# Two pairs' input loads moved behind a weight piece, and matmul units re-cut, in a linear-attention and MLP kernel

## The chip, the cores and the metric

The kernel runs on one core of a Trainium2 chip. A core has a matrix engine (TensorE, PE in the profile; its weight loads are listed as PEld), VectorE (DVE), ScalarE (ACT), GpSimd (POOL) and SyncE (SP, which only issues DMAs and waits). They run side by side, each through its own instructions in order, and wait for each other by semaphores. Sixteen DMA engines move data between DRAM and the on-chip memory. The metric is the device time of one execution in microseconds (us); less is better.

## The reference

The inputs are q, k, v of shape (4, 8, 768, 64) in float32, a decay `lam` per head, a gain `g_ln` and two weight matrices, W1 (512 x 2048) and W2 (2048 x 512). First comes attention with decay, in blocks of 64 positions with a running state, then a layer norm and a two-layer MLP with a residual:

```python
for b in range(nb):                      # blocks of 64 positions
    intra = einsum('bhic,bhjc->bhij', qb, kb) * Dmask      # Dmask: lam ** (i - j), lower triangle
    intra = einsum('bhij,bhjd->bhid', intra, vb)
    inter = einsum('bhid,bhde->bhie', qb * lam_pow, kv_state)
    out[:, :, sl] = intra + inter
    kv_state = lam_block * kv_state + einsum('bhsd,bhse->bhde', kb * rev_pow, vb)
x = out as (4, 768, 512)
xn = (x - mean) / sqrt(var + 1e-6) * g_ln
result = x + relu(xn @ w_ch1) @ w_ch2
```

## The kernel before

The 4 x 768 positions are cut into twelve windows of 256, numbered 0 to 11; a window is a pair of 128-row tiles, so "the fourth pair" is window 3 and "the fifth" window 4. A window goes through these stages:

- loads of k, q, v (512 KB each) into buffers `kin`, `qin`, `vin`, of which there are three per name; SP issues them (L76, later L80). `open_in` names the buffers; with its second argument true, POOL first writes one element of the k buffer (L91), so that the loads, which write the same buffer, wait for POOL to get that far;
- casts and scalings to bf16 (`in_k`, `in_q`, `in_v`; L218 to L245) on ACT, DVE or POOL;
- transposes of k and q to `kqT`, on PE for windows 0 to 2 (L253), by DMA from SP for the later ones (L260);
- scores (L282), masking, state products (L316), new states (`new_state`; POOL's decay is L322), attention output (L428, L441) and the norm;
- the transpose of the normed rows to `xT`, on PE (L502) or by DMA, and then the MLP of this window, called a group.

The MLP is cut into units. The first product x W1 makes 16 hidden blocks of 128 for the group's two tiles. A whole unit, `m1(n)`, takes two hidden blocks for both tiles: eight matmuls of 256 columns (L539). A split unit, `m1.tile(c, i)`, takes four hidden blocks for tile i alone: sixteen matmuls of 128 columns (L650). Both do the same arithmetic, fill one bank of the accumulation memory and are drained by one ACT instruction (L542, L653). Eight units of either kind make a group. The second product is `m2(i, part)` for groups 0 to 3 (four matmuls of 512 columns, L676), where part 0 to 3 reads piece 0 to 3 of W2; the later groups use a product scheme with fewer multiplications (L574).

W1 and W2 come in four pieces each, cast on the way by DMAs that POOL issues (`load_w1`, L117; `load_w2`, L120). `behind(tile)` is a copy of one column by POOL (L737), so that whatever follows on POOL's queue stands behind the landing of that tile.

The order is written out by hand. Each engine runs its instructions in the order of the program text. `plan` is a list of the units from group 1's second half on, and `units(n)` issues the next n of them between the attention steps. The order around the change, before it: POOL issues the last two pieces of W2, writes the gate element for window 3, scales v of window 2 and decays two states; SP issues k, q, v of window 3 and k, q of window 4; then PE goes through window 2's transposes, the first units of the plan and window 2's scores.

At the start of the program PE does 36 small matmuls into a tile `unread` (L180), whose values nothing reads, in a loop of 18 with two each.

Of the kernel before, what the change touches and what calls it, by code (L numbers as in the profile page):

```python
# [17 lines left out]
def kernel(  # L18
# [11 lines left out]
    nc = tc.nc  # L30
# [41 lines left out]
    def fill(got, name, u, hs, eng=None):  # L72
        eng = eng or nc.sync
        src = dict(k=k, q=q, v=v)[name]
        if u < LB:
            eng.dma_start(got[:, hs], source(src, u, hs))  # L76
            return
        cc, b = divmod(u, B)
        for j in range(2):
            eng.dma_start(got[:, hs, j * D:(j + 1) * D],  # L80
                          src[b, hs, cc * W + j * C:cc * W + (j + 1) * C, :].rearrange("h p d -> p h d"))
# [6 lines left out]
    def open_in(u, gate):  # L88
        qkv_in[u] = {name: inp.tile([128, H, 2 * D], F32, tag=name + "in", name=name + "in") for name in "kqv"}
        if gate:  # L90
            nc.gpsimd.memset(qkv_in[u]["k"][:, 0, 0:1], 0.0)  # L91

    def load_in(u, name, eng):
        got = qkv_in[u][name]
        fill(got, name, u, slice(0, H), eng)
        qkv_in[u][name] = got.rearrange("p h (j d) -> p h j d", j=2)
# [14 lines left out]
    w2 = [const.tile([128, KB // NWC, DM], F16, name=f"w2_{c}") for c in range(NWC)]  # L111
# [7 lines left out]
    def load_w2(c):  # L119
        nc.gpsimd.dma_start(w2[c], moe_w_ch2[c * W2K * 128:(c + 1) * W2K * 128, :].rearrange("(k p) d -> p k d", p=128))  # L120
# [54 lines left out]
    nc.vector.memset(ones, 1.0)  # L175
    nc.vector.tensor_copy(keep64[half[1]], keep64_b[half[1]])
    unread = ps.tile([128, 32], F32, tag="po0", name="unread")
    for _ in range(18):
        for b in range(2):
            nc.tensor.matmul(unread[half[b]], lhsT=ident[half[0], half[b]], rhs=ident[half[0], 0:32],  # L180
                             start=True, stop=True, skip_group_check=True)
# [60 lines left out]
    def in_v(u, eng, hs=ALL):  # L242
        n = hs.stop - hs.start
        lv = lam_v[:, hs, :, None] if u < LB else lam_p[:, 1, hs, None, None]
        eng.tensor_tensor(st[u]["vb"][:, hs], qkv_in[u]["v"][:, hs], lv.to_broadcast([128, n, 2, D]), op=ALU.mult)  # L245
# [75 lines left out]
    def decay(eng, dst, src):  # L321
        eng.tensor_tensor(dst, src, lam_s[:, :, None].to_broadcast([128, NP, D]), op=ALU.mult)  # L322

    def state_sum(u, ab):
        tmp = wk.tile([128, NP, D], F32, tag="Stmp", name="Stmp")
        nc.vector.tensor_tensor(tmp, st[u]["pk"][ab], state[u % B], op=ALU.add)
        return tmp

    def new_state(u, ab, eng):

        s = st[u]
        b = u % B
        if ab == 1 and len(s["pk"]) == 1:
            return
        old = state.get(b)
        if ab == 0:
            s["S"] = [(old, old)]
        Sn = wk.tile([128, NP, D], BF16, tag="S", bufs=12, name="Sn")
        if old is None and eng is nc.scalar:
            for p in range(NP):  # L340
                nc.scalar.activation(Sn[:, p], s["pk"][ab][:, p], ACT.Identity, scale=lam_s[:, p:p + 1])
        elif old is None:
            decay(nc.vector, Sn, s["pk"][ab])
        else:
            tmp = s.pop("tmp", None) or state_sum(u, ab)
            decay(eng, Sn, tmp)
        state[b] = Sn
        if ab == 0:
            s["S"].append((Sn, Sn))
# [384 lines left out]
    def behind(tile_ap):  # L734

        seen_p = wk.tile([128, 1], F32, tag="seen_p", name="seen_p")
        nc.gpsimd.tensor_copy(seen_p, tile_ap)  # L737
# [47 lines left out]
    m1b, m2b = mlp(1)  # L785
# [41 lines left out]
    def s1b(u):  # L827
        scores(u, 0)
        mask(u, 0)
# [194 lines left out]
    keep_x(1, nc.scalar.copy)  # L1024
    load_w2(2)
    load_w2(3)
    open_in(3, True)
    in_v(2, nc.gpsimd)
    load_in(3, "k", nc.sync)
    load_in(3, "q", nc.sync)  # L1030
    load_in(3, "v", nc.sync)
    open_in(4, False)
    load_in(4, "k", nc.sync)
    load_in(4, "q", nc.sync)
    plan = [(m1b.tile, c, i) for c in (2, 3) for i in range(2)]
    plan += [(m2, i, part) for part in range(KB // 4) for m2, i in ((m2a, 0), (m2a, 1), (m2b, 0))]
    plan += [(m2b, 1, part) for part in range(KB // 4)]
    for g in range(2, len(groups)):
        m1, m2 = mlp(g)
        plan += [(m1.tile, 0, 0), (m1.tile, 0, 1)] if g == 2 else [(m1, 0), (m1, 1)]  # L1040
        plan += [(m1, n) for n in range(2, m1.count)]
        if g >= WG:
            plan += [(m2.w, n) for n in range(8)]
        else:
            plan += [(m2, i, part) for i in range(len(groups[g])) for part in range(KB // 4)]
# [3 lines left out]
    def units(n):  # L1049
        for _ in range(n):  # L1050
            f, *a = next(steps)
            f(*a)
# [4 lines left out]
    transpose_pe(2, 1, (0, 1, 2, 3))  # L1057
    new_state(0, 1, nc.gpsimd)
    new_state(1, 1, nc.gpsimd)
    units(2)  # L1060
    s1b(2)
    units(2)
# [310 lines left out]
```

## Time and profile before

| | |
|---|---|
| median of 5 runs | 209.07 us (208.81 to 209.25) |
| the profiled execution | 209.25 us; its span from the first to the last instruction 207.5 us |
| PE | 198.5 us busy (96%), 3199 matmuls |
| PEld | 159.9 us (77%) |
| DVE, ACT, POOL | 133.8 us (65%), 120.7 us (58%), 84.5 us (41%) |
| HBM read and written | 27.27 MB and 6.29 MB, 162 GB/s over the span |
| granted PE clock | 0.997 |

Busy time is the time in which an engine had at least one instruction running. PE's matmuls are pipelined and the profile models their ends, so the time that one matmul takes in a stream is read from start to start and not from its listed length. Times in a timeline row are the start and the length, counted from the first instruction; brackets give the idle time before the row and who ended it. DMA share is the mean busy share of the 16 DMA engines; in a short stretch it can exceed 1, since a packet's whole time is counted where it starts.

### The profile page before, as it was taken

What the parts mean: (1) busy time and instruction counts of PE and PEld (TensorE: products, weight loads), DVE (VectorE), ACT (ScalarE), POOL (GpSimd) and SP (SyncE); (2) the same over time, 40 slices, a digit from 0 to 9 for tenths busy, and PEclk for the clock granted to TensorE, in tenths of its full rate; (3) what the DMA queues carried; (4) which work ended last, traced back from release to release, by engine and by line L of the source; (5) the groups of instructions that cost most, each with busy time, mean ns of one, the idle gap of its engine ahead of it and who ended that gap; (6) DMA issues with size and microseconds to landing.
All of it is one profiled execution on the core that took longest, in us unless ns stands there. A gap on an engine that the chain in (4) does not pass through costs nothing.

```text
span 207.5 us, 7435 instructions
## 1 busy us (share of the span) xinstructions
PE 198.5 (96%) x3199; PEld 159.9 (77%) x3199; DVE 133.8 (65%) x277; ACT 120.7 (58%) x278; POOL 84.5 (41%) x117
## 2 busy tenths in 40 slices
PE   4988999999999999999999999999999999999991
PEld 2477889655785586588888888888888888988881
DVE  2586481525964459867888774766876947865252
ACT  3775578726258358257565775585596565652620
POOL 5658049016946342365264441782282202001020
PEclk9999999999999999999999999999999999999998
DMA  4999999999998999999999999797968020158403
GB/s 106 303 255 212 171 287 174 206 267 274 160 264 216 255 186 180 189 243 197 212 207 121 192 208 160 202 202 153 196 124 176 3 51 0 29 122 269 144 16 90
DMA packets 91011, 36.41 MB, mean 175 GB/s; under 512 B 65121, under 2 KB 88161, under 8 KB 90978
## 3 DMA queue, kind: packets, MB, share of 16 engines
q1 hardware_dynamic: 86368, 31.53, 74.6%
q0 software_dynamic: 4224, 4.19, 12.7%
q8 instruction: 25, 0.41, 0.9%
q10 hardware_dynamic: 386, 0.20, 0.4%
q14 instruction: 8, 0.07, 0.1%
HBM read 27.27 MB, written 6.29 MB: 162 GB/s over the span
## 4 chain that ended last, share of the span: by engine, by line
PE 88%; ACT 3%; DMA 3%; DVE 2%; SPq 1%; issue 1%; POOLq 0%; POOL 0%; DVEq 0%
PE pm L539 36%; PE pm L676 14%; PE pm1t L650 6%; PE pwd L574 6%; PE pwa L574 6%; PE pwc L574 6%; PE pwb L574 3%; DMA qin<-in_q_dram 3%; PE po L441 2%; PE tp L253 2%; PE po L428 2%; PE xt L502 1%; DVE x L587 1%; PE po L415 1%; PE sc L362 1%; PE sc L282 1%
## 5 line engine op out<-in xcount | busy, mean ns | idle before, releaser
L539 PE MATMUL pm<-xT,w 128*128 128x256 bf16 x672 | 76.9, 273 | 0.0
L539 PEld LDWEIGHTS <-w 128*128 128x128 bf16 x672 | 64.6, 98 | 8.3 <-DVE Smid L397 0.3
L542 ACT ACTIVATE hT<-pm 128x512 f16<-128x512 f32 x84 | 49.2, 596 | 24.8 <-PE pm L539 24.7
L676 PE MATMUL pm<-w,hT 128*128 128x512 f16 x128 | 29.8, 380 | 0.0
L574 PEld LDWEIGHTS <-hs 128*128 128x128 f16 x256 | 24.9, 98 | 2.9
L599 POOL TENSOR_TENSOR x<-ev_u,x 128x256 f32<-128x256 f32 x8 | 5.8, 724 | 51.4 <-ACT ev_u L598 40.0
L557 DVE TENSOR_TENSOR hs<-hT 128x1024 f16<-128x1024 f16 x16 | 14.0, 873 | 16.1 <-ACT hT L542 16.0
L322 POOL TENSOR_TENSOR Sn<-Stmp,lam_s 128x256 bf16<-128x256 f32 x16 | 9.8, 616 | 33.3 <-DVE Stmp L400 15.5
L676 PEld LDWEIGHTS <-hT 128*128 128x128 f16 x128 | 11.7, 98 | 12.5
L574 PEld LDWEIGHTS <-hT 128*128 128x128 f16 x192 | 18.8, 98 | 2.2
L469 DVE SCALAR_TENSOR_TENSOR xc<-po,nmean,g_row 128x512 bf16<-128x512 f32 x18 | 13.0, 746 | 4.9 <-ACT nmean L468 4.8
L467 ACT ACTIVATE x<-po 128x512 f32<-128x512 f32 x18 | 10.6, 590 | 7.9 <-PE po L441 4.5
L650 PE MATMUL pm1t<-xT,w 128*128 128x128 bf16 x192 | 13.6, 234 | 0.7 <-ACT kqT L254 0.6
L650 PEld LDWEIGHTS <-w 128*128 128x128 bf16 x192 | 12.5, 106 | 1.7 <-DMA w<-in_moe_w_ch_dram 0.9
L245 POOL TENSOR_TENSOR vb<-vin,lam_v 128x1024 bf16<-128x1024 f32 (+1 forms) x7 | 11.6, 1660 | 5.2 <-DMA vin<-in_v_dram 5.2
L512 ACT ACTIVATE sq<-x,nmean 128x512 bf16<-128x512 f32 x18 | 12.9, 719 | 0.3
L653 ACT ACTIVATE hT<-pm1t 128x512 f16<-128x512 f32 x12 | 7.3, 605 | 9.9 <-PE pm1t L650 9.8
L292 DVE TENSOR_TENSOR mA<-sc,keep 128x512 bf16<-128x512 f32 x14 | 9.0, 684 | 5.1 <-PE sc L282 5.1
L245 POOL TENSOR_TENSOR vb<-vin,lam_p 128x1024 bf16<-128x1024 f32 x6 | 11.4, 1896 | 2.0 <-ACT hT L542 1.9
L587 DVE SCALAR_TENSOR_TENSOR x<-pwd,rstd,x 128x256 f32<-128x256 f32 x16 | 7.7, 482 | 3.6 <-POOL x L607 3.6
L239 POOL TENSOR_TENSOR kq<-qin,lam_p 128x512 bf16<-128x512 f32 x9 | 9.3, 1042 | 1.7 <-DMA qin<-in_q_dram 1.7
L587 DVE SCALAR_TENSOR_TENSOR x<-pwa,rstd,x 128x512 f32<-128x512 f32 (+1 forms) x16 | 9.1, 612 | 0.8
(134 smaller groups left out, 317.2 us busy)
## 6 DMA issues: line engine op xcount, KB each, us to landing
out_dram<-x SPq DMA_DIRECT2D x22, 256.0 KB, 3.9
w<-in_moe_w_ch_dram POOLq DMA_DIRECT2D x8, 512.0 KB, 8.3
kin<-in_k_dram SPq DMA_DIRECT2D x14, 256.0 KB, 5.6
qin<-in_q_dram SPq DMA_DIRECT2D x14, 256.0 KB, 4.9
vin<-in_v_dram SPq DMA_DIRECT2D x14, 256.0 KB, 4.8
kin<-in_k_dram SPq DMA_DIRECT2D x5, 512.0 KB, 7.9
qin<-in_q_dram SPq DMA_DIRECT2D x5, 512.0 KB, 6.6
vin<-in_v_dram SPq DMA_DIRECT2D x5, 512.0 KB
```

The costliest lines, as they stand in the source:

```text
L245: eng.tensor_tensor(st[u]["vb"][:, hs], qkv_in[u]["v"][:, hs], lv.to_broadcast([128, n, 2, D]), op=ALU.mult)
L322: eng.tensor_tensor(dst, src, lam_s[:, :, None].to_broadcast([128, NP, D]), op=ALU.mult)
L467: nc.scalar.activation(x, po, ACT.Copy, accum_out=sm)
L469: nc.vector.scalar_tensor_tensor(xc, in0=po, scalar=nm, in1=g_row, op0=ALU.add, op1=ALU.mult)
L512: nc.scalar.activation(sq, s["x"][:, ab], ACT.Square, bias=s["nmean"][:, ab:ab + 1], accum_out=ss[:, ab:ab + 1])
L539: nc.tensor.matmul(pm[:, b, :], lhsT=w1[n // W2K][:, kk, (n % W2K) * 128:(n % W2K + 1) * 128], rhs=xT_of[g][:, kk, 0:N], start=(b == 0 and ...
L542: nc.scalar.activation(hT[:, u * NB:(u + 1) * NB, 0:N], pm, ACT.Relu)
L557: nc.vector.tensor_tensor(s13, b[:, :, 1:2, :].to_broadcast([128, n, 2, 128]), b[:, :, 0:4:3, :], op=ALU.subtract)
L574: nc.tensor.matmul(pr[bank], lhsT=lhs(r), rhs=rhs, start=(first and r == 0), stop=(r == KB // 2 - 1), skip_group_check=True)
L587: nc.vector.scalar_tensor_tensor(out, in0=in0, scalar=r[ab], in1=in1, op0=ALU.mult, op1=ALU.add)
L650: nc.tensor.matmul(pm[:, b, :], lhsT=w1[c][:, kk, b * 128:(b + 1) * 128], rhs=xT_of[g][:, kk, i * 128:(i + 1) * 128], start=(b == 0 and kk ...
L676: nc.tensor.matmul(acc[i], lhsT=hT[:, kk, i * 128:(i + 1) * 128], rhs=w2[kk // W2K][:, kk % W2K, :], start=(kk == 0), stop=(kk == KB - 1))
```

## The change

It has three parts.

- The loop of `unread` runs 16 times instead of 18: 32 matmuls instead of 36.
- The plan's units are cut otherwise. Group 1's second half was four split units and becomes four whole ones. Group 2's first two units were split and become whole. Group 3's last four units were whole and become split. The number of units stays the same.
- The gate and the loads of window 3 and of k and q of window 4 move down in the text, behind window 2's transposes, the first unit and POOL's two state decays, and a `behind` is put before them, so that on POOL's queue the gate stands behind the landing of W2's second piece. `in_v(2)` stays ahead of it. The definition of the plan moves up, which has no effect of its own.

```diff
-    for _ in range(18):
+    for _ in range(16):
         for b in range(2):
             nc.tensor.matmul(unread[half[b]], ...
...
     load_w2(2)
     load_w2(3)
+    in_v(2, nc.gpsimd)
+    plan = [(m1b, n) for n in range(m1b.count // 2, m1b.count)]
+    plan += [(m2, i, part) for part in range(KB // 4) for m2, i in ((m2a, 0), (m2a, 1), (m2b, 0))]
+    plan += [(m2b, 1, part) for part in range(KB // 4)]
+    for g in range(2, len(groups)):
+        m1, m2 = mlp(g)
+        if g == 3:
+            plan += [(m1, n) for n in range(4)] + [(m1.tile, c, i) for c in (2, 3) for i in range(2)]
+        else:
+            plan += [(m1, n) for n in range(m1.count)]
...
+    transpose_pe(2, 0, (0, 1, 2, 3), nc.vector)
+    units(1)
+    transpose_pe(2, 1, (0, 1, 2, 3))
+    new_state(0, 1, nc.gpsimd)
+    new_state(1, 1, nc.gpsimd)
+    behind(w2[1][:, 0, 0:1])
     open_in(3, True)
-    in_v(2, nc.gpsimd)
     load_in(3, "k", nc.sync)
     load_in(3, "q", nc.sync)
     load_in(3, "v", nc.sync)
     open_in(4, False)
     load_in(4, "k", nc.sync)
     load_in(4, "q", nc.sync)
-    plan = [(m1b.tile, c, i) for c in (2, 3) for i in range(2)]
...
-        plan += [(m1.tile, 0, 0), (m1.tile, 0, 1)] if g == 2 else [(m1, 0), (m1, 1)]
-        plan += [(m1, n) for n in range(2, m1.count)]
...
-    transpose_pe(2, 0, (0, 1, 2, 3), nc.vector)
-    units(1)
-    transpose_pe(2, 1, (0, 1, 2, 3))
-    new_state(0, 1, nc.gpsimd)
-    new_state(1, 1, nc.gpsimd)
     units(2)
     s1b(2)
```

More of the change, by code (lines that the diff above doesn't have):

```diff
@@ L1026 @@
     load_w2(3)
-    open_in(3, True)
     in_v(2, nc.gpsimd)
[L1029 to L1034, printed above, removed]
-    plan = [(m1b.tile, c, i) for c in (2, 3) for i in range(2)]
+    plan = [(m1b, n) for n in range(m1b.count // 2, m1b.count)]
     plan += [(m2, i, part) for part in range(KB // 4) for m2, i in ((m2a, 0), (m2a, 1), (m2b, 0))]
@@ L1059 @@
     new_state(1, 1, nc.gpsimd)
+    behind(w2[1][:, 0, 0:1])
+    open_in(3, True)
+    load_in(3, "k", nc.sync)
+    load_in(3, "q", nc.sync)
+    load_in(3, "v", nc.sync)
+    open_in(4, False)
+    load_in(4, "k", nc.sync)
+    load_in(4, "q", nc.sync)
     units(2)
```

## The prediction

> **What bounds the kernel now.** I read the page first, then the list of what TensorE (PE) waited for, then the timelines of PE, GpSimd (POOL) and SyncE (SP) around the edit, then the DMA share in stretches of 2 us.
>
> From the page: the span, and the shares of the chain that ended last.
>
> ```profile
> span 207.5 us, 7435 instructions
> PE 88%; ACT 3%; DMA 3%; DVE 2%; SPq 1%; issue 1%; POOLq 0%; POOL 0%; DVEq 0%
> ```
>
> PE is the chain. Its waits over the whole run (waiter, releaser, us in total, times, longest):
>
> ```profile
> PE g_all L183 <- DMA g_one<-in_moe_g_ln_dram: 1.6, 1, 1.6
> PE unread L180 <- POOL ident L132: 1.4, 1, 1.4
> PE pm1t L650 <- ACT kqT L254: 0.6, 1, 0.6
> ...
> ```
>
> Three more rows of 0.2 each close that list, and all six waits lie before 17 us. From 17 to 197 us PE waits for nothing the list resolves, so this change can help only by removing PE work or by changing what happens in the first 22 us, and can hurt only by making PE wait for something that now comes in time.
>
> PE around the edited units (start, length, line, shape, count):
>
> ```profile
> 35.03 1.95 PE L650 MATMUL pm1t<-xT,w 128*128 128x128 bf16 x32
> 36.91 0.42 PE L282 MATMUL sc<-kqT 64*64 64x128 bf16 x16
> ...
> 54.38 1.95 PE L650 MATMUL pm1t<-xT,w 128*128 128x128 bf16 x32
> 56.17 1.91 PE L539 MATMUL pm<-xT,w 128*128 128x256 bf16 x16
> ...
> ```
>
> The 32 matmuls of two split units (L650) start at 54.38 and hand over at 56.17: 1.79 us, 55.9 ns each, 0.895 us a unit. Further on, 32 matmuls of four whole units (L539) start at 76.65 and hand over at 80.16: 3.51 us, 0.878 a unit. Split and whole units cost PE almost the same.
>
> POOL, on whose queue the new wait goes:
>
> ```profile
> 31.90 1.55 POOL L120 DMA_DIRECT2D w<-in_moe_w_ch_dram  x2
> 33.43 0.12 POOL L91 MEMSET kin<- 128x1 f32 x1
> 33.49 1.92 POOL L245 TENSOR_TENSOR vb<-vin,lam_v 128x1024 bf16<-128x1024 f32 x1
> 35.36 1.18 POOL L322 TENSOR_TENSOR Sn<-Stmp,lam_s 128x256 bf16<-128x256 f32 x2
> 41.84 0.61 POOL L322 TENSOR_TENSOR Sn<-Stmp,lam_s 128x256 bf16<-128x256 f32 x1 [5.30 <-DVE rstd L517]
> ```
>
> SP, which issues the moved loads:
>
> ```profile
> 33.58 0.37 SPq L76 DMA_DIRECT2D kin<-in_k_dram  x1
> ...
> 34.77 7.60 SPq L76 DMA_DIRECT2D vin<-in_v_dram  x1
> 42.46 3.55 SPq L76 DMA_DIRECT2D kin<-in_k_dram  x1
> 46.06 1.55 SPq L76 DMA_DIRECT2D qin<-in_q_dram  x1
> 48.45 5.30 SPq L260 DMA_TRANSPOSE kqT<-kq  x2
> ```
>
> The 7.60 and 3.55 us are issues held back by transfers that do not drain. The stretches (last two columns: DMA share, GB/s) say why:
>
> ```profile
> 34.00:36.00 2.00, 2.00 (x40) 2.00 (x38) 0.58 (x1) 2.00 (x5) 2.00 (x3) 1.00 1.18 177
> 36.00:38.00 2.00, 2.00 (x48) 1.80 (x45) 0.63 (x2) 1.51 (x3) 0.54 (x1) 1.00 1.15 188
> 42.00:44.00 2.00, 2.00 (x79) 1.10 (x77) 0.00 (x0) 0.00 (x0) 0.46 (x1) 1.00 1.19 215
> 46.00:48.00 2.00, 2.00 (x18) 1.02 (x19) 0.78 (x2) 0.89 (x3) 0.62 (x2) 1.00 1.22 306
> ```
>
> The DMA engines are full (share over 1) from 32 to 52 us. The rate shows what runs: about 183 GB/s while W2 moves alone (its rate is counted in its half-width destination), about 306 with the q/k/v loads alone, 215 when mixed.
>
> **The change, part by part.** The sum is made against the profiled execution, 209.25 us (span 207.5 plus 1.75 around it). The median of the five runs is 209.07, so I take 0.18 off.
>
> *Unread matmuls, 36 to 32.* They run 1.43 to 2.57 us, a pair every 0.053 us: 2 pairs, 0.11 us less. PE then sits idle 1.55 us for g_one until 4.12, which hides it: 0. Without that cover it would be a gain of 0.11.
>
> *Split against whole units.* The four units of m1b and the first two of group 2 become whole, the last four of group 3 become split: six fewer, four more, net two. 2 x (0.895 - 0.878) = -0.03 us. ScalarE drains one 128x512 bank per unit either way (605 ns split at L653, 596 whole at L542). A whole unit needs both halves of xT: group 1's transposes ran at 27.3 and 29.5, against a unit at 33.69; group 2's at 47.9 and 49.0, against 54.38. No wait. Splitting group 3's second half leaves its W2 products fed: the first of them needs hidden blocks 0 to 3, from units 0 and 1.
> The Trainium skill, "TensorE: Matmul & The Clock Gate", section "Back-to-back issue gap", gives about 81 ns a matmul for N=128 in a real stream of weight loads and matmuls; an estimate by that page makes a split unit 16 x 81 = 1.30 us and the net saving 0.84 us, the sum 208.2. The row above measures 55.9 ns, and the sum goes by the row.
>
> *POOL's order.* in_v(2) starts 0.06 earlier, the two state decays end at 36.5, then POOL waits for W2's second piece. That piece is issued at 29.94 and, by the view of tile w, lands 7.9 later, at 37.8; nothing ahead of it changes. The copy takes 0.19 (the same copy at L737), the gate memset 0.12: 38.1. Next on POOL's queue is the decay at 41.84, which waits for VectorE anyway. The cover is 3.7 us, so: 0. If W2's piece came later than 41.5, PE's use of that state at 43.84 would be late by the excess less 1.4.
>
> *The loads on SP.* SP reaches them at 38.2 instead of 33.58. Behind them in its queue are only the transposes of the fourth pair at 48.45 (they wait for VectorE's half of k) and what follows. The first k load is issued at 33.58 and, by the view of tile kin, lands 12.6 later, at 46.2. But at 34 to 38 us the rate is that of W2 alone (177, 188): the early issue gets it nothing until about 37. From 38 to 44 the mix of 215 splits as 183f + 306(1-f), f = 0.74: a quarter of the engines' time is the loads', about 80 GB/s. Holding them until their first packets, some 2 us after 38.2, takes 3 us x 0.26 = 0.8 us of engine time from them and gives it to W2, whose last piece then lands 0.8 earlier (33.45 - 0.75 + 13.3 = 46.0 now). The engines never run dry, so the loads get it back: k lands between 46.2 (all given back) and 47.0 (none). I take 46.3, as the full share in all stretches is nearest to the first. The other four loads stand behind it in the same full pipe and shift no more.
> The Trainium skill, "DMA: Bandwidth & Descriptors", section "Queues, rings and completion order", says that each DMA engine takes turns between the queues that have work. By that, an estimate is that the loads had half the engines from 35 us on, and the delay would be some 2 us, which still leaves the sum where it is. The rows of 34 to 38 us do not show such turns.
>
> *What a later k meets.* By the view of tile kqT the transposes land at 55.0 and 55.7 (issued 48.45 and 52.46, landing 6.5 and 3.3 later) and PE's scores of this pair start at 58.28: 2.5 us of slack. For the fifth pair they land at 66.7 and scores start at 70.51: 3.8. So 0 to 0.8 us later costs 0. W2's pieces were not waited for either: the third lands at 42.0 and is first read at about 45, the fourth at 46.0 and is read at 48.11; landing earlier is worth 0.
>
> Sum: 209.25 - 0.03 - 0.18 = 209.04, so **209.0 us**. With the bounds (0.11 at the start, 0.2 either way for run to run, which is half the 0.44 between the fastest and slowest run) the likeliest case covers 208.7 to 209.4.
>
> **The rivals.**
>
> *Late loads (slower).* If issue order did decide and the loads moved by the whole 4.6 us, k lands at 50.8. The first transpose then starts 0.42 (VectorE's copy) later at 51.3 instead of 48.45, 2.8 late; the pair's q is cast on POOL (2.22 us for two), which puts the second transpose up to 4.6 late, landing at 58.5 to 60.3 against 58.28. PE stalls 0.2 to 2.0 us there, and SP's later loads follow. Price: 209.3 to 211.1, middle 210.2. It decides once the transposes slip more than 2.5 us. Against it: the 34-to-38 rows. For it: SP's queue is serial and hardly idle after 48 us.
>
> *The first 22 us (either side).* The first two L650 units take 1.89 and 1.82 us, later ones 0.9: PE runs at half pace until about 22.0. No row shows what ends it. If the four missing matmuls move that point, each us is worth 0.5 us. PE's stretch without a wait starts at 16.7, so at the earliest the gain is 5.3 / 2 = 2.6 us; I price it at one us either way of a likely move of 2: 208.0 or 210.0. PE's 0.64 us idle before 16.73, where the weight loads wait for W1's first piece, is of the same kind, within 0.6. Against it: the removed 0.11 us lies 14 us ahead of that stretch, behind another idle time.
>
> *Split units cost more than their start times show (faster).* Each has 8 extra weight loads of 98 ns. If these were exposed, two units fewer give 2 x 8 x 0.098 = 1.6 us: 207.5. Against it: 55.9 ns from start to start already contains them.
>
> *The change does nothing* is, in time, my forecast.
>
> **How the numbers follow.** A measurement of this kernel can tell about 0.2% (0.4 us) from no change. Forecast 0.50 (same). Late loads 0.17, slower. First 22 us later 0.08, slower; earlier 0.17, faster. Split units 0.08, faster. So faster 0.25, same 0.50, slower 0.25. The range leaves out the 0.08 below and the upper half of the late loads above: 208.0 to 210.2.
>
> **What would show it.** In the new profile: on POOL a copy ending near 38.0 and the memset after it; on SP the first k load at 38.2, landing 8 to 9 us later; W2's last piece landing near 45; the transposes within 1 us of 48.45 and 52.46; PE's wait list still without a row behind 17 us; whole units at 33.7 to 37 of 0.88 us. Wrong would be: a PE wait for kqT, vb or DMA between 57 and 90 us (late loads), or the first full-pace matmul more than 0.4 us away from 22.0.

## The result, and the profile after

The changed kernel takes 209.99 us (median of 39 runs, 208.61 to 212.66) against 208.99 us (median of 65 runs, 207.66 to 210.31) for the one before: ratio 1.0048, 95% interval 1.0035 to 1.0061. It is 1.0 us slower. Here and below, ratios leave out executions in a slower state of the chip; of this kernel's these are the ones of 212.43 and 212.66 us, and without them the slowest took 211.11. The profiled execution took 210.21 us with a span of 208.5.

The page of the changed kernel, span and PE's share:

```profile
span 208.5 us, 7396 instructions
PE 198.0 (95%) x3179; PEld 158.9 (76%) x3179; DVE 132.4 (64%) x277; ACT 120.9 (58%) x278; POOL 84.7 (41%) x118
```

PE works 0.5 us less and the span is 1.0 us longer, so PE stands somewhere. Its list of waits has one new row that matters:

```profile
PE g_all L183 <- DMA g_one<-in_moe_g_ln_dram: 1.7, 1, 1.7
PE unread L180 <- POOL ident L132: 1.4, 1, 1.4
PE pm L539 <- DVE Smid L397: 1.3, 1, 1.3
```

It is the only row behind 17 us, and the timeline puts it at 149 us, 110 us after the edit of the loads. First PE, then its weight loads, around it:

```profile
148.02 1.05 PE L539 MATMUL pm<-xT,w 128*128 128x256 bf16 x8
150.34 6.29 PE L539 MATMUL pm<-xT,w 128*128 128x256 bf16 x56 [1.27 <-DVE Smid L397]
...
150.33 6.01 PEld L539 LDWEIGHTS <-w 128*128 128x128 bf16 x56 [1.54 <-issue]
```

Eight matmuls of a whole unit start at 148.02, 0.109 us apart, so the ninth was due at 148.90. It starts at 150.34: 1.43 us lost, from start to start. The same place in the profile of before has no such hole:

```profile
148.61 2.56 PE L539 MATMUL pm<-xT,w 128*128 128x256 bf16 x22
```

Two things in these rows speak against the named releaser. The weight load reads only W1, which landed 120 us earlier, and it stands too, put down to "issue": no semaphore in the profile explains it. And VectorE's `Smid` (149.34 to 149.76 in its timeline), which could have freed the new unit's bank, ends 0.58 us before PE goes on.

Up to there the changed kernel was ahead. The first L676 unit behind group 3's first product starts at 79.78 (80.16 before): 0.38 ahead. Of that, 0.34 was there at the first full-pace matmul (21.72 against 22.06), which is an accident of the execution (the last section has its range over all profiles), and 0.04 is what the re-cut saves. 1.43 - 0.38 = 1.05 us is the loss in the span.

The rest of the profile answers point by point to what was shown of before. POOL, the new wait and its cover:

```profile
33.42 1.92 POOL L245 TENSOR_TENSOR vb<-vin,lam_v 128x1024 bf16<-128x1024 f32 x1
35.29 1.18 POOL L322 TENSOR_TENSOR Sn<-Stmp,lam_s 128x256 bf16<-128x256 f32 x2
37.59 0.18 POOL L737 CAST seen_p<-w 128x1 f32<-128x1 f16 x1 [1.11 <-DMA w<-in_moe_w_ch_dram]
37.70 0.10 POOL L91 MEMSET kin<- 128x1 f32 x1
41.42 0.61 POOL L322 TENSOR_TENSOR Sn<-Stmp,lam_s 128x256 bf16<-128x256 f32 x1 [3.62 <-DVE rstd L517]
```

SP, the moved loads and the transposes behind them:

```profile
37.83 0.37 SPq L76 DMA_DIRECT2D kin<-in_k_dram  x1
...
48.03 4.75 SPq L260 DMA_TRANSPOSE kqT<-kq  x2
```

k is issued 4.25 us later and lands 8.3 us after that (12.6 before), at 46.1 against 46.2. The transposes start 0.4 earlier than before. W2's last piece lands at 44.4 instead of 46.0. This part cost nothing, as forecast. One step on the way was other than worked out: the first packet of k moves 3.8 us after the issue (37.83 to 41.59), where some 2 us were taken, and in the kernel before it was 3.6 us (33.58 to 37.19). So the empty wait moved along with the loads.

### The profile page after: what moved, and what is told of

Its sections match the earlier page's. It is cut to its first block, busy times and chain, and to the rows that moved or that the text cites. A ratio compares the mean times of both kernels' runs of the same rounds, so it can differ in the third digit from the quotient of the medians.

```text
span 208.5 us, 7396 instructions
## 1 busy us (share of the span) xinstructions
PE 198.0 (95%) x3179; PEld 158.9 (76%) x3179; DVE 132.4 (64%) x277; ACT 120.9 (58%) x278; POOL 84.7 (41%) x118
## 4 chain that ended last, share of the span: by engine, by line
PE 85%; ACT 3%; issue 3%; DMA 3%; DVE 2%; POOL 1%; SPq 1%; POOLq 0%; DVEq 0%; ACTq 0%
PE pm L539 36%; PE pm L676 14%; PE pwc L574 5%; PE pwa L574 5%; PE pm1t L650 5%; PE pwd L574 5%; PE pwb L574 3%; DMA qin<-in_q_dram 3%; PE po L441 2%; PE tp L253 2%; PE po L428 2%; PE xt L502 1%; DVE x L587 1%; PE sc L282 1%; PE po L415 1%
## 5 line engine op out<-in xcount | busy, mean ns | idle before, releaser
L539 PE MATMUL pm<-xT,w 128*128 128x256 bf16 x688 | 79.2, 273 | 1.3 <-DVE Smid L397 1.3
L539 PEld LDWEIGHTS <-w 128*128 128x128 bf16 x688 | 66.0, 98 | 10.2 <-issue 1.5
L542 ACT ACTIVATE hT<-pm 128x512 f16<-128x512 f32 x86 | 50.9, 597 | 31.8 <-PE pm L539 31.7
L676 PE MATMUL pm<-w,hT 128*128 128x512 f16 x128 | 29.8, 380 | 0.0
L557 DVE TENSOR_TENSOR hs<-hT 128x1024 f16<-128x1024 f16 x16 | 12.7, 796 | 19.0 <-ACT hT L542 19.0
L676 PEld LDWEIGHTS <-hT 128*128 128x128 f16 x128 | 11.7, 98 | 12.5
L574 PEld LDWEIGHTS <-hT 128*128 128x128 f16 x192 | 18.8, 98 | 2.2
L650 PE MATMUL pm1t<-xT,w 128*128 128x128 bf16 x160 | 11.0, 234 | 0.7 <-ACT kqT L254 0.6
L650 PEld LDWEIGHTS <-w 128*128 128x128 bf16 x160 | 10.3, 106 | 1.4 <-DMA w<-in_moe_w_ch_dram 0.9
L574 PE MATMUL pwa<-w,hT 128*128 128x256 f16 x64 | 9.6, 273 | 0.0
```

The costliest lines, as they stand in the source:

```text
L539: nc.tensor.matmul(pm[:, b, :], lhsT=w1[n // W2K][:, kk, (n % W2K) * 128:(n % W2K + 1) * 128], rhs=xT_of[g][:, kk, 0:N], start=(b == 0 and ...
L542: nc.scalar.activation(hT[:, u * NB:(u + 1) * NB, 0:N], pm, ACT.Relu)
L557: nc.vector.tensor_tensor(s13, b[:, :, 1:2, :].to_broadcast([128, n, 2, 128]), b[:, :, 0:4:3, :], op=ALU.subtract)
L574: nc.tensor.matmul(pr[bank], lhsT=lhs(r), rhs=rhs, start=(first and r == 0), stop=(r == KB // 2 - 1), skip_group_check=True)
L650: nc.tensor.matmul(pm[:, b, :], lhsT=w1[c][:, kk, b * 128:(b + 1) * 128], rhs=xT_of[g][:, kk, i * 128:(i + 1) * 128], start=(b == 0 and kk ...
L676: nc.tensor.matmul(acc[i], lhsT=hT[:, kk, i * 128:(i + 1) * 128], rhs=w2[kk // W2K][:, kk % W2K, :], start=(kk == 0), stop=(kk == KB - 1))
```

## The cause, as the experiments will show it

PE's instructions come from DRAM in packets of 16 KB on a DMA queue that the page calls "q8 instruction": 25 packets, 0.41 MB, in both kernels. That the queue is PE's is worked out from the count: a matmul is two instructions, the weight load and the multiplication, and 3199 matmuls of the kernel before are 6398 instructions, 256 a packet. Here is the DMA view of the changed kernel for 147.5 to 148.9 us:

```profile
q1 hardware_dynamic: 1125, 0.28, 117.8%
q8 instruction: 1, 0.02, 5.8%
```

That one packet starts at 147.54 and ends at 148.84, in the middle of the last window's k and v loads on q1. PE goes on 1.50 us after its end.

Which instruction PE stood at can be counted. 2523 matmuls of the trace had started before the hole: 5046 instructions. The trace holds 11 semaphore and drain instructions of PE ahead of it as well. If 63 more that it does not hold (the start of the program) stand ahead, 74 in all, the sum is 5120 = 20 x 256. This was the 19th packet on q8. So theory A was: PE holds two blocks of 256 instructions (256 x 64 bytes are the 16 KB); the packet for block 20 is asked for about when PE enters block 19, and must be there when block 19 is through. How long that takes depends on what block 19 holds. The attention stage of a window is some 120 matmuls on 64 rows, which PE starts in 1.2 us. In the changed kernel block 19 begins exactly with that stage, and block 20 is due 2.1 us after its entry (by the start times of before, counted 20 matmuls on). In the kernel before, block 19 begins 20 matmuls of 0.109 us earlier, and it is 3.3 us.

The 20 matmuls are what the change took out ahead of this place: 4 unread, 32 in group 1, 16 in group 2, less the 32 that group 3 got. Two rivals: theory B, the moved loads push later transfers, so that a bank comes free late, as the wait list says; theory C, the re-cut units cost in themselves.

## The experiments

Each ratio is to the kernel before, run on the same chip. The stalls are from one profile each, from start to start, less the usual distance.

**One part alone: the loads.** The kernel before with

```diff
-    open_in(3, True)
...
+    behind(w2[1][:, 0, 0:1])
+    open_in(3, True)
+    load_in(3, "k", nc.sync)
...
```

and the five loads moved as in the change.

> The kernel before with only the loads moved behind W2's second piece; 36 unread matmuls and the units as before. Theory A (TensorE stands at 148.8 us because its instructions come in blocks of 256 and the 20th block, fetched on DMA queue q8, is asked for too late; what counts is how many instructions stand ahead of that block): the count is that of before, so no stall of TensorE over 0.3 us behind 17 us, ratio 1.000 +- 0.002. Theory B (the moved loads push SyncE's later transfers so that VectorE frees an accumulation bank late, as the wait list names DVE Smid): the stall of 1.3 to 1.5 us near 149 us is there, ratio 1.005. Theory C (the re-cut units): nothing, ratio 1.000.

Measured: 0.999 (0.9964 to 1.0016), no stall near 149 us. Theory B falls. It has a stall that A's expectation had excluded, 0.70 us at 62.5 us, at matmul 990, where the profile of before has 0.07: 2 x 990 + 68 = 8 x 256, the start of block 8. (68 is the same 63 and the 5 semaphore and drain instructions up to there.)

**The change with its count restored.** The changed kernel with

```diff
-    for _ in range(16):
+    for _ in range(26):
```

> The changed kernel with 52 unread matmuls at the start instead of 32: 20 matmuls, 40 instructions more, which lie in TensorE's idle time before 4.1 us and bring every block boundary behind 80 us back to where it is in the kernel before. Loads and units stay as changed. Theory A: no stall near 149 us, ratio to before 1.000 +- 0.002, that is 1.0 us faster than the changed kernel for 20 useless matmuls more. Theory B and C: the stall stays, ratio 1.005.

Measured: 1.0029 (1.0001 to 1.0057). The stall near 149 us is gone, by 20 useless matmuls. In time the gain is not shown: this interval and that of the change, 1.0035 to 1.0061, overlap. PE's waits behind 17 us are now

```profile
PE po L428 <- issue: 0.9, 1, 0.9
PE pm L539 <- DMA w<-in_moe_w_ch_dram: 0.8, 1, 0.8
```

The second is a wait for a piece of W1 until 21.73 us, which the profile of the change does not have. The first is at matmul 990, 1.05 us from start to start. At that early place the pad does not restore the count of before (group 3's split units, which add 32, come later), and there block 8 is due 4.7 us after the entry of block 7, against 5.0 before. So the stalls fit the block theory, and my expectation of 1.000 looked at one block only.

**The kernel before with 20 matmuls less at the start.**

```diff
-    for _ in range(18):
+    for _ in range(8):
```

> The kernel before with 16 unread matmuls instead of 36, loads and units as before: 20 matmuls less at the start, so that the 20th block begins at the same place as in the changed kernel. Theory A: a stall of 1.0 to 1.8 us in the first product's units (L539) behind the tenth window's attention stage, q8's packet ending some 1.5 us before TensorE goes on, ratio 1.004 to 1.007. Theory B and C: no stall, ratio 1.000.

Measured: 1.009 (1.0054 to 1.0125), more than expected. PE in this run:

```profile
148.40 1.05 PE L539 MATMUL pm<-xT,w 128*128 128x256 bf16 x8
150.92 1.26 PE L539 MATMUL pm<-xT,w 128*128 128x256 bf16 x10 [1.47 <-DVE xc L469]
```

The hole is again behind the eighth matmul of the unit and matmul 2523 of the run: 148.40 + 8 x 0.109 = 149.27, so 1.65 us, and the packet had ended at 149.42, 1.50 before PE went on. Another 0.70 us stands at matmul 990. The expected 1.004 to 1.007 counted block 20 alone; the two together are 2.35 us, 1.1% of the time. Loads and units are those of before; leaving out work that lies in idle time reproduces the loss. The named releaser is now another VectorE instruction, `xc`.

**One part alone: the units.** The kernel before with the plan of the change.

> The kernel before with only the units re-cut as in the change; 36 unread matmuls and the loads as before: 16 matmuls, 32 instructions less ahead of the 20th block. Theory A: that block is needed four matmuls (0.4 us) earlier in the program than in the changed kernel and is also asked for 0.4 us earlier, so the same stall of 1.0 to 1.8 us, ratio 1.004 to 1.007. Theory B (loads): no stall, ratio 1.000. Theory C (the cut itself costs): ratio 1.005, but with the loss between 33 and 80 us.

Measured: 1.0012 (0.9984 to 1.0039). The stall at matmul 2523 is there, four matmuls earlier in the unit as expected, but 0.64 us; another 0.40 at matmul 990, and 0.50 at 121.6 us at no block's start, for which I have no explanation. In this execution the packet started 0.10 us before PE entered block 19, where in the changed kernel it started 0.73 after. Theory C falls, since between 33 and 80 us nothing is lost but the 0.40 at block 8. In time this part alone shows no loss, where 1.004 to 1.007 was expected.

**One part alone: the unread matmuls.** The kernel before with 16 in place of 18.

> The kernel before with 32 unread matmuls instead of 36, loads and units as before. Theory A (blocks of 256 instructions): every block begins 4 matmuls later; the stretch between entering block 19 and needing block 20 shrinks from 3.3 to 2.9 us, where the changed kernel has 2.1; a stall of 0 to 0.4 us there, ratio 0.999 to 1.002. Were the unread matmuls to act in themselves (start of the clock, first 22 us): the whole 1.005.

Measured: 0.9985 (0.9957 to 1.0013); no stall at block 20, 0.28 us at block 8. Neither this part nor the loads is slow alone.

**The change without the moved loads.** Plan and unread count as changed, loads as before.

> The changed kernel with the loads back where they were: 32 unread matmuls and the re-cut units. Theory A: the same count as the changed kernel, so the stall of 1.0 to 1.8 us at block 20 (matmul 2523 of the run), ratio 1.003 to 1.007. Theory B (moved loads): no stall, 1.000.

Measured: 1.0034 (1.0004 to 1.0064), stalls of 0.71 us at matmul 2523 and 0.44 at 990. The loss does not need the loads. The count of instructions is that of the changed kernel and the stall is half of its 1.43 us; here the packet started 0.13 us before block 19 was entered. Whether the four unread matmuls add something to the re-cut is not settled: 1.0012 and 1.0034 have overlapping intervals.

**The same instructions, less traffic.** The changed kernel with

```diff
-    load_in(11, "k", nc.sync)
+    qkv_in[11]["k"] = qkv_in[10]["k"]
...
-    load_in(11, "v", nc.sync)
+    qkv_in[11]["v"] = qkv_in[10]["v"]
```

> The changed kernel, but the last window's k and v are not loaded (its casts read the window before's buffers, so that window's part of the result differs): 1 MB less traffic at 142 to 149 us, all instructions of TensorE as in the changed kernel. If the instruction block is late because it queues behind the loads, q8's packet starts and ends earlier and the stall at block 20 falls from 1.43 to below 0.9 us, ratio to before 0.998 to 1.003. If the fetch takes a fixed time from the asking, the stall stays at 1.2 to 1.6 us, ratio 1.005.

Measured: 0.9982 (0.9951 to 1.0012). The stall at matmul 2523 is 0.31 us. From 142 to 149 us the core moves 121 GB/s instead of 221, and the packet starts 0.42 us before block 19 is entered, not 0.73 after. It takes as long as before, 1.29 us against 1.30, so what changed is its start. One start in one profile proves little, since with all loads it also came 0.10 and 0.13 us early in the runs with the re-cut units alone and without the moved loads. The median of twelve runs says more: with the same instructions it lies below the change's, and from the end of the hole to the end of the span the two profiles take the same time within 0.4 us. The kernel before holds the other case, a short block without traffic. Its block 21 is used up in 2.2 us (161.17 to 163.35) without a hole: q1 moves nothing from 159.64 to 166.64, and the packet starts 0.85 us before the block is entered and ends 1.9 us before the next one is due. So the block is late for two reasons together: it is due soon, and its packet starts late while the DMA engines are full. That the packet stands in a queue behind the loads is the likely way, but no view shows it.

**Away from both boundaries.** The kernel before with 26 in place of 18.

> The kernel before with 52 unread matmuls instead of 36: every block begins 16 matmuls earlier. Theory A: entering block 7 to needing block 8 grows from 5.0 to 6.5 us, entering block 19 to needing block 20 from 3.3 to 4.8 us, so neither stalls; ratio 0.996 to 1.000 (block 8 cost 0.07 us in the one profile of before and up to 0.7 in other kernels). Without theory A: 1.000, or a little above it for more matmuls.

Measured: 1.0001 (0.9975 to 1.0028). PE's list of waits is empty behind 17 us and no block stalls there; the profiled span is 206.6 us. Ahead of that the start of block 2 holds PE for 0.6 us until 16.03, which costs nothing: the first unit starts at 16.68, against 16.73 before. It was the candidate for a better kernel, but the median does not show it. What before loses at its own boundaries may be too little or too rare to be seen so.

**A stall put where there was none.** The kernel before with 41 in place of 18.

> The kernel before with 82 unread matmuls instead of 36, all still inside TensorE's idle time before 4.1 us. Theory A: blocks 8 and 20 get 6.3 and 7.8 us between the entry of the block before and their own first instruction (5.0 and 3.3 before), so no stall there; but block 12 now begins with the attention stage near 92 us and block 13 is needed 2.9 us after that (7.6 before), while a fetch in this stretch takes about 5.4 us from the entry: a new stall of 0.5 to 2.5 us near 94 us, at matmul 1629 give or take 3, ratio 1.002 to 1.010. If more unread matmuls simply help or do nothing: 1.000 or below, no stall there.

Measured: 1.0106 (1.0068 to 1.0145), the slowest of all, though its 46 extra matmuls lie in idle time. The stall is at matmul 1629 to the matmul:

```profile
90.85 0.30 PE L441 MATMUL po<-Sn,kqT 64*64 64x64 bf16 x16
92.66 4.54 PE L539 MATMUL pm<-xT,w 128*128 128x256 bf16 x40 [1.51 <-ACT nmean L468]
...
92.65 4.37 PEld L539 LDWEIGHTS <-w 128*128 128x128 bf16 x41 [1.62 <-issue]
```

2 x 1629 + 70 = 13 x 256. The packet ended at 91.12 and PE went on 1.54 us later, 1.59 us late. Blocks 8 and 20 did not stall, as expected; blocks 4 and 15 did, by 0.57 and 0.31, which I had not looked at. The trace names ScalarE this time. The three stalls add up to 2.5 us, 1.2% of the time.

**Second profiles of both kernels.**

> The kernel before, a second profile, for the spread between executions. Theory A: no stall at block 20 (matmul 2523 of the order), at block 8 (matmul 990) 0 to 0.7 us, each time with q8's packet ending 1.3 to 1.6 us before TensorE goes on.

> The changed kernel, a second profile. Theory A: a stall of 0.6 to 1.8 us at matmul 2523, TensorE going on 1.5 to 1.65 us after q8's packet ends. If the first profile's stall was an accident of that execution: none.

Measured: the changed kernel stalls at the same matmul again, by 1.69 us, with PE going on 1.47 after the packet:

```profile
147.21 1.05 PE L539 MATMUL pm<-xT,w 128*128 128x256 bf16 x8
...
149.78 0.22 PEld L539 LDWEIGHTS <-w 128*128 128x128 bf16 x3 [1.80 <-issue]
```

The kernel before has nothing at blocks 8 and 20, but 0.85 us at a third place, matmul 1245 (2 x 1245 + 70 = 10 x 256):

```profile
74.61 0.22 PE L441 MATMUL po<-Sn,kqT 64*64 64x64 bf16 x2 [0.68 <-issue]
```

So the kernel before has such holes too, at a changing place and size. The change moved a block's start to a place where a hole comes in all six profiles of the kernels whose block 20 begins in this unit, by 0.31 to 1.69 us.

**All profiles together.** The runs above show sixteen stalls of 0.28 to 1.69 us, at the starts of blocks 4, 8, 10, 13, 15 and 20. Counted with the same 63 instructions and the semaphore and drain instructions of each trace, every one of them lies within one instruction of a multiple of 256. And at none of the 312 starts of blocks 2 to 25 in the thirteen profiles does PE begin sooner than 1.27 us after the end of the block's packet.

Six other waits of 0.2 us or more stand in the lists behind 17 us, at no block's start: 0.8 us for W1 in the changed kernel with its count restored and in the one with less traffic (until 16.86), 0.2 with 82 unread matmuls, 0.4 and 0.3 for VectorE's `hs` (L557) at 143.6 with 32 unread matmuls and at 142.0 in the second profile of the change, and the one at 121.6 named above, 0.3 in its list. By their names they are waits for data; why they come in some profiles only stays open.

## Why the prediction was wrong

The forecast was 209.0 us and no change that can be measured, with half the chance. The time is 1.0 us more than before. 209.99 lies in the range given, and the slower side had a quarter of the chance, but for reasons that did not occur: that it lies there is luck.

- *What bounds the kernel:* right, PE. That it can lose only by waiting for "something that now comes in time" was right in words; I looked for that something among data and banks alone.
- *Unread matmuls at 0 and the re-cut at -0.03:* as work these terms were right; the profile shows the 0.04. The step that failed is that both were costed as work only. They also take 40 instructions out of PE's stream ahead of block 20, and that term, missing from the sum, was 1.43 us in the profiled execution. Leaving out 20 unread matmuls alone, which is 0 by the prediction's reckoning since they lie in idle time, cost 0.9%. The page of before shows 25 packets on q8, and the distance of 256 instructions can be counted from it.
- *POOL's order at 0:* right. The wait ended at 37.6, and POOL's next work was at 41.42.
- *The loads:* k landed 0.1 us earlier, where 46.3 was taken; the engines stayed full. Right in the landing, wrong in one step: the first packet came 3.8 us after the issue and not some 2. The loads got all of it back, since W2's last piece landed 1.6 us earlier and not 0.8. The estimate from the skill of a delay of some 2 us did not happen: q1 moved nothing from the issue to 41.59.
- *Late loads (rival):* right in sign, wrong in mechanism; with the loads alone the ratio is 0.999. (Its 50.8 + 0.42 is 51.2, not 51.3, which changes nothing.)
- *Split units cost more (rival):* did not occur; the profile shows 0.04 saved, and with the re-cut units alone the ratio is 1.0012.
- *First 22 us (rival):* not seen as a cause. The two L650 units that the prediction gives as 1.89 and 1.82 us take 1.68 and 1.66 from start to start. PE reached full pace at 22.0 and 19.0 in the two profiles of before, 21.3 and 18.0 in those of the change. In the other nine it was between 18.8 and 22.7. The kernels with 32 unread matmuls alone lie anywhere from 18.0 to 22.7, so single profiles show no effect of the count.
- *What would show it wrong:* I named a wait for kqT, vb or a DMA between 57 and 90 us. The wait came at 149 us under the name of a VectorE instruction.

The Trainium skill, "Runtime: NRT & Kernel Launch", section "Instruction fetch mechanics", says that engines refill their instructions in blocks of 16 KB, 256 instructions, and the runs agree. It gives PE room for 2048 instructions, though a note in the same section speaks of two lines of 16 KB, and calls the cost of crossing a block mostly hidden. Here the 19th packet was awaited at the start of block 20, as with room for two blocks, and the crossing cost 0.3 to 1.7 us where it showed. The measurement decides.

## What to carry to other kernels

An edit that adds or removes instructions on the busiest engine shifts every later instruction against its fetch blocks; count on in steps of 256 instructions, and look at where a block begins just ahead of a burst of short instructions while the DMA engines are full. When PE stands, its weight load says "issue" and the named releaser changes from run to run, count the instructions before you believe the name. Useless instructions in an idle stretch can move the boundary, for better (the changed kernel with 52 unread matmuls lost its stall at 149 us, though its time is not shown to be less) or for worse (82 of them cost the kernel before 1%).

## What the runs showed of the hardware

- PE goes on 1.3 to 1.7 us after the end of the packet with its next instructions, in every stall at a block's start, and never sooner than 1.27 us at any of 312 block starts. In bursts a block of 256 instructions is used up in 2.2 us (161.17 to 163.35 in the kernel before).
- Beside POOL's W2 pieces, the first packet of a k load moved 3.6 us after SP issued it at 33.58, and 3.8 us after the issue at 37.83; for the load issued at 23.69, beside W1, it was 1.0 us. What sets this delay, no run here shows. Issued 4.25 us later, k landed at the same time.
- PE runs at half pace until a time between 18.0 and 22.7 us that changes from execution to execution of the same kernel. At 0.5 us of span for 1 us that is up to 2.3 us, an estimate, against 2.65 us between the fastest and the slowest run of the kernel before; so two single profiles can differ by it without a reason in the code.
